# Sparse attention and a maxout layer on one core: turning transfers from two queues, the first batch's key sums kept apart, weights by quarters, a new order of the work

## The chip, the core and the metric

The kernel runs on one core of a Trainium2 chip. A core has five engines that run side by side, each taking its own instructions strictly in order: TensorE (PE; its weight loads are listed apart as PEld), VectorE (DVE), ScalarE (ACT), GpSimd (POOL) and SyncE (SP). Transfers between the chip's memory and the core's buffers are issued by SP, and in part by ACT, and are carried by 16 DMA engines. The metric is the device time of one execution in microseconds; lower is better.

## The reference, cut to what matters

Four batches of eight heads, 768 positions, 64 values per head. Each query sees the keys within 15 positions of its own, and beside them 24 summaries of 32 keys each (the maximum over the 32 keys, and the mean of the 32 values). The output of the attention, 512 numbers for each of 3072 positions, goes through a layer that takes the larger of two products and multiplies once more.

```python
k_sum = k.reshape(B, H, nb, block, D).max(axis=3)
v_sum = v.reshape(B, H, nb, block, D).mean(axis=3)
mask_l = np.abs(pos[:, None] - pos[None, :]) < window
scores_all = np.concatenate([where(mask_l, scores_l, -1e9), scores_s + np.log(block)], axis=-1)
a = softmax(scores_all)
x = matmul(a, concat([v, v_sum]))          # then (B*S, H*D)
out = np.maximum(x @ w1, x @ w2) @ w_out   # w1, w2: 512 x 1024, w_out: 1024 x 512
```

The kernel writes the maximum as h1 + max(h2 - h1, 0): it multiplies x by wd = w2 - w1, cuts at zero (g), and adds x times the product w1o = w1 w_out, which it forms once.

## The kernel before, in words

The unit of attention is a tile of 64 queries (16 rows further on than a multiple of 64) against 128 rows of keys: 96 neighbours and 32 rows that hold the 24 sums. Even tiles take their keys and values in one order of those rows, odd tiles in another. Two heads lie side by side (a "pair", hp 0 to 3), two pairs make a half (hp 0 or 2), and four tiles make a group (grp 0 to 2, 256 positions). Names carry batch, pair and group: "values 121" is batch 1, half 2, group 1.

For each batch and pair `prep` (L599 to L671) casts k and q to 16 bits (tile kqb), turns them so that the head dimension lies on the partitions, and places k in the tile kx with its neighbours, its sums (ks, made by a maximum on DVE) and copies of the tails. Pairs named in `turn` (22, 23, 30 to 33) are turned by a transposing transfer (L628, into kt), the others by TensorE (L624). `scores` (L673) fills a bank pair, `weigh` (L711) takes the exponential on ACT and hides what is out of the window (a multiplication on DVE; in the first batch a matrix product beforehand, "hide", L690), `values` (L741) multiplies by the values and divides (tile xs), and x is turned into xt: by TensorE in the first batch (L831), by a transposing transfer in the others (L822). `maxout` (L904) makes four "hidden" tasks of eight products each per group (L913), cuts them at zero on ACT or DVE ("relu"), and six "out" steps of four products each (L940 with w1o, L947 with w_out), whose banks a "copy out" empties before a store.

The weights: `load_w12` (L844) loads rows 0 to 255 or 256 to 511 of half of the columns of w1 and w2, forms that part of wd, and turns w1. A hidden task needs both row halves of its columns. `load_wo` loads w_out.

Everything is put on record as tasks, and a table in `CFG` sets the order in which they are written out (`given`, L247): one list of task numbers, one letter for each task's engine, and a list of the buffer slots. The order is thus by hand for each engine, nothing is reordered on the chip, and an instruction that waits holds all that stands behind it on its engine. The recording layer puts in the waits. Transfers count on eight counters in turn (DMAHW0 to DMAHW7), and a transfer waits for the one that used its counter before.

```python
if by_dma:
    op("S", 1.12, lambda e, src=src, ps=ps: nc.sync.dma_start_transpose(out=ps.ap[:], in_=src.ap[:]),
       read=[src], write=[ps], prio=prio, issue=1.24, label=f"turn {'kq'[n]}{tag}")
```

PSUM has eight banks. A hidden task or an out step that begins takes one, and starts only when the relu, the copy out or the exponential that read its last contents has run.

Of the kernel before, what the change touches and what calls it, by code (L numbers as in the profile page):

```python
# [27 lines left out]
    turn="22 23 30 31 32 33", lx="SSS", cols=True, emb=1, ep=0.5, vt=0.28, s32=0.36, raw=0, qg=0, wh=1, os=6,  # L28
)
CFG["order"] = list(map(int, """  # L30
# [204 lines left out]
def kernel(  # L235
# [32 lines left out]
    def tiles(name, n, shape, dt):  # L268
        return [const.tile(shape, dt, name=f"{name}{i}") for i in range(n)]


    banks = Ring(list(range(8)), {"kq": 2, "sc": -2, "av": -2, "mm": 4})
    bank_tile = psum.tile([128, 8, 512], F32, name="banks")

    def bank(buf, n=512, dt=F32, second=0):
# [54 lines left out]
    def fixed_parts():  # L330
# [24 lines left out]
        def clear_apart(e):  # L355

            for t in apart:
                zero(e, t[:])
# [701 lines left out]
```

## Time and profile before

| | us |
|---|---|
| median of the runs shown (three) | 165.5 (164.76 to 165.97) |
| the profiled execution | 166.2 |
| its span, first to last instruction | 164.4 |
| PE busy | 153.0 |
| DVE / ACT / POOL busy | 113.0 / 92.9 / 57.8 |

The granted TensorE clock was 1.000 over the whole span. The profiled execution took 0.7 us more than the median; 1.8 us of it lie outside the span. In the rows of the profile each line gives a start, a duration, the engine and what it did; "idle before <- X" says that the engine stood still until X had ended, and for a transfer "landing" is counted from its issue.

### The profile page before, as it was taken

How to read it: one execution, taken by the hardware profiler on the slowest of the kernel's cores; microseconds unless marked ns; L12 is line 12 of the kernel's file. 1: busy time of each engine (PE TensorE's matmuls, PEld its weight loads, DVE VectorE, ACT ScalarE, POOL GpSimd, SP SyncE). 2: the span in 40 equal slices, each digit the busy share in tenths (PEclk: the TensorE clock that was granted, in tenths of full speed). 3: DMA queues.
4: the chain of work that ended last, by engine and by line, in shares of the span. 5: the costliest groups of instructions: out<-in, count | busy, mean ns of one | idle time of the engine just before them, and what ended most of it. 6: DMA issues, size and time to landing. Idle time of an engine off the chain costs nothing.

```text
span 164.4 us, 4431 instructions
## 1 busy us (share of the span) xinstructions
PE 153.0 (93%) x1793; PEld 100.2 (61%) x1812; DVE 113.0 (69%) x224; ACT 92.9 (57%) x134; POOL 57.8 (35%) x91
## 2 busy tenths in 40 slices
PE   5889978999999999999999999999899999999992
PEld 2346657998565644575687646678545467766651
DVE  3698898579856899994989986569746654163221
ACT  3469995794577698836996645283937312012010
POOL 6058757302242385534672546034630000000000
PEclk9999999999999999999999999999999999999999
DMA  5999999999999999999979997997999996311015
GB/s 157 289 331 303 273 386 383 383 382 371 274 190 289 271 233 219 130 232 136 201 169 229 228 209 162 121 261 150 220 245 335 319 174 167 58 64 70 0 66 189
DMA packets 67700, 36.46 MB, mean 222 GB/s; under 512 B 54624, under 2 KB 61664, under 8 KB 67680
## 3 DMA queue, kind: packets, MB, share of 16 engines
q1 hardware_dynamic: 66208, 33.76, 87.6%
q10 hardware_dynamic: 1472, 2.43, 4.4%
q8 instruction: 14, 0.23, 0.6%
q14 instruction: 6, 0.05, 0.1%
HBM read 25.17 MB, written 6.29 MB: 191 GB/s over the span
## 4 chain that ended last, share of the span: by engine, by line
PE 62%; DMA 14%; DVE 11%; issue 4%; SPq 4%; ACT 2%; POOL 1%; ACTq 0%; POOLq 0%; DVEq 0%
PE banks L913 19%; PE banks L947 17%; PE banks L940 10%; DMA land<-in_k_dram 8%; DMA out_dram<-o 6%; PE banks L897 4%; PE banks L624 3%; PE banks L757 3%; DVE vx L593 3%; PE banks L701 2%; PE banks L982 2%; DVE ks L650 2%; DVE pb L725 2%; DVE kqb L593 1%; SPq L428 1%
## 5 line engine op out<-in xcount | busy, mean ns | idle before, releaser
L913 PE MATMUL banks<-xt,wd 128*128 128x256 bf16 x384 | 45.9, 273 | 0.1
L947 PE MATMUL banks<-wo,g 128*128 128x512 bf16 (+2 forms) x194 | 43.4, 362 | 1.8 <-issue 1.6
L913 PEld LDWEIGHTS <-wd 128*128 128x128 bf16 x384 | 37.3, 98 | 7.8 <-issue 0.5
L947 PEld LDWEIGHTS <-g 128*128 128x128 bf16 x208 | 18.7, 98 | 17.3
L715 ACT ACTIVATE pb<-banks 128x1024 bf16<-128x1024 f32 x24 | 23.6, 1026 | 6.2 <-PE banks L701 3.8
L940 PE MATMUL banks<-w1o,xt 128*128 128x512 bf16 (+2 forms) x100 | 23.5, 362 | 0.2
L922 ACT ACTIVATE g<-banks 128x512 bf16<-128x512 f32 x27 | 15.2, 604 | 7.6 <-PE banks L913 7.6
L924 DVE TENSOR_SCALAR g<-banks 128x512 bf16<-128x512 f32 x21 | 14.1, 686 | 7.8 <-PE banks L913 7.6
L816 DVE TENSOR_TENSOR xs<-banks,inv 128x512 bf16<-128x512 f32 x24 | 16.0, 686 | 4.9 <-DMA xt<-xs 4.4
L593 POOL COPY vx<-sums 32x792 bf16<-32x792 bf16 x15 | 14.7, 983 | 12.5 <-ACT sums L593 7.0
L725 DVE TENSOR_TENSOR pb<-pb,mask 128x1024 bf16<-128x1024 bf16 (+1 forms) x24 | 16.4, 710 | 4.0 <-ACT pb L715 3.7
L593 ACT COPY o<-banks 128x512 f32<-128x512 f32 (+1 forms) x8 | 4.4, 546 | 25.6 <-PE banks L947 21.1
L593 POOL CAST kqb<-land 128x768 bf16<-128x768 f32 x9 | 8.9, 985 | 20.1 <-DMA land<-in_q_dram 9.8
L940 PEld LDWEIGHTS <-xt 128*128 128x128 bf16 x104 | 9.9, 98 | 9.4
L650 DVE TENSOR_REDUCE ks<-kx 128x24 bf16<-128x768 bf16 x16 | 15.0, 945 | 0.2
L593 DVE COPY o<-banks 128x512 f32<-128x512 f32 (+2 forms) x10 | 6.2, 621 | 10.2 <-PE banks L947 8.7
L593 POOL CAST vx<-land 128x768 bf16<-128x768 f32 x10 | 8.9, 889 | 10.2 <-DMA land<-in_v_dram 10.2
L593 ACT CAST kqb<-land 128x768 bf16<-128x768 f32 x11 | 10.3, 943 | 3.2 <-DMA land<-in_k_dram 2.5
L593 DVE CAST kqb<-land 128x768 bf16<-128x768 f32 x12 | 7.0, 590 | 7.1 <-DMA land<-in_k_dram 4.7
L624 PE MATMUL banks<-ident,kqb 128*128 128x128 f32 x60 | 9.7, 278 | 1.4 <-DVE kqb L593 1.1
L757 PEld LDWEIGHTS <-pb 128*64 128x64 bf16 (+1 forms) x384 | 8.0, 110 | 4.9 <-issue 2.8
L757 PE MATMUL banks<-vx,pb 128*64 128x65 bf16 (+1 forms) x384 | 9.5, 196 | 1.3 <-DVE xs L816 0.8
(87 smaller groups left out, 183.1 us busy)
## 6 DMA issues: line engine op xcount, KB each, us to landing
land<-in_k_dram SPq DMA_DIRECT2D x16, 384.0 KB, 6.0
land<-in_v_dram SPq DMA_DIRECT2D x16, 384.0 KB, 6.9
land<-in_q_dram SPq DMA_DIRECT2D x16, 384.0 KB, 5.9
land<-in_moe_w_dram SPq DMA_DIRECT2D x8, 512.0 KB, 9.6
land<-in_moe_w_out_dram SPq DMA_DIRECT2D x4, 512.0 KB, 10.0
out_dram<-o SPq DMA_DIRECT2D x7, 256.0 KB, 4.0
out_dram<-o ACTq DMA_DIRECT2D x4, 256.0 KB, 2.8
out_dram<-w1t SPq DMA_DIRECT2D x3, 256.0 KB, 3.4
```

Source lines behind the costliest of these rows:

```text
L593: {"D": nc.vector.tensor_copy, "A": nc.scalar.copy, "P": nc.gpsimd.tensor_copy}[e](out=o, in_=i)
L624: nc.tensor.transpose(out=bank(ps)[:, 128 * j:128 * j + 128], in_=src.ap[:].bitcast(F32)[:, 128 * j:128 * j + 128], identity=ident32[:])
L650: op("D", 0.95, lambda e: nc.vector.tensor_reduce(out=ks.ap[:, 0:nb], in_=free(kt(), 128, [256, NM], [192, 2], [32, 2], [1, 32]), axis=AX. ...
L715: op("A", {"A": 1.03}, lambda e: nc.scalar.activation(out=spread(pb.ap[:, 0, 0:1], [192, 8], [128, 2], [1, 64]) if PW > 128 else spread(pb ...
L725: nc.vector.tensor_tensor(out=o, in0=o, in1=spread(mask[:, 2 * u:2 * u + 1, 0:1], [0, n], [64, 2], [1, 64]), op=ALU.mult)
L757: nc.tensor.matmul(out=o, lhsT=p[r], rhs=vx[b].ap[r, par, hp + n, 2 * grp + u, a, 0:D + 1], start=(PW == 128 or par == 0), stop=(last and ...
L816: op("D", 0.69, lambda e: nc.vector.tensor_tensor(out=x.ap[:].rearrange("p n u a d -> p n (u a) d"), in0=spread(bank_tile[:, ps.ap, 0:1], ...
L913: nc.tensor.matmul(out=bank(ps)[:, 256 * s:256 * s + 256], lhsT=wd_tile[:, quarter, c, 128 * s:128 * s + 128], rhs=x.ap[:, c, :], start=(c ...
L922: nc.scalar.activation(out=o, in_=bank(ps), func=ACT.Relu)
L924: nc.vector.tensor_scalar_max(out=o, in0=bank(ps), scalar1=0.0)
L940: nc.tensor.matmul(out=bank(ps, c1 - c0), lhsT=x.ap[:, c, sl], rhs=w1o[c].ap[:, cols], start=(c == 0), stop=False)
L947: nc.tensor.matmul(out=bank(ps, c1 - c0), lhsT=g.ap[:, f, sl], rhs=wo[f // 2].ap[:, f % 2, cols], start=False, stop=(f == FC - 1))
```

## The change

Four things change together with the table of the order.

1. **Turning transfers from ACT.** The transposing transfers for k and q (L628) and for x (L822) may be issued by ACT instead of SP. The new letters give ACT 11 of the 30: six of x and five of k and q.
2. **First batch.** Keys are placed in one run of 768 columns plus a tail of 32, with no copies of the tails and no copies of the sums. The sums are multiplied apart: after a group's 96-row products, `scores` adds products with ks into rows 96 to 127 of the same banks. Odd tiles use the same order of rows as even ones, so one tile `apart` holds the sums of the values where two did, and one mask without the odd form (hide0) does for them.
3. **First weights by quarters.** Of the four parts of w1 and w2, parts 1 and 3 become a quarter of the columns with all 512 rows each (`load_w12_quarter`), so a hidden task of these columns needs one part. Parts 0 and 2 stay halves of rows.
4. **A new order, new engines and new slots** for all tasks. Beside these, several options come in switched off (`f32`, `mx1`).

```diff
-    turn="22 23 30 31 32 33", lx="SSS", cols=True, emb=1, ep=0.5, vt=0.28, s32=0.36, raw=0, qg=0, wh=1, os=6,
+    turn="22 23 30 31 32 33", lx="SSS", cols=True, emb=1, ep=0.5, vt=0.28, s32=0.36, raw=0, qg=0, wh=2, os=6, f32="", ft=0.7, mx1=0, ksep=1, sd=0.56,
...
-44 32 2 0 3 10 12 1 4 6 11 15 13 8 112 20 30 26 56 25 46 113 116 9 122 7 123 126 14 47 16 117 34 118 132 168 28 23 133
+5 10 11 8 0 9 17 13 3 6 2 1 21 26 45 56 33 24 27 126 14 18 118 46 35 34 127 31 12 119 29 23 130 122 110 120 121 32 174
...
-                op("S", 1.12, lambda e, src=src, ps=ps: nc.sync.dma_start_transpose(out=ps.ap[:], in_=src.ap[:]),
+                op("S", {"S": 1.12, "A": 1.12}, lambda e, src=src, ps=ps: queue(e).dma_start_transpose(out=ps.ap[:], in_=src.ap[:]),
...
+        apart_k = CFG["ksep"] and b == 0
...
-            pairs(128, 192, 64), order(kps, [1, 128], [128, 6]) if by_dma else order(kps, [2, 128], [256, 3], [1, 2])),
+            kt()[:, 0:S] if apart_k else pairs(128, 192, 64), order(kps, [1, 128], [128, 6]) if by_dma else order(kps, [2, 128], [256, 3], [1, 2])),
...
+        if not apart_k:
+            copy(tail_on, {"D": 0.26, "P": 0.51, "A": 0.55}, lambda: (
+                pairs(192, 64, 32), pairs(320, 64, 32)),
+               read=[kmain, kwrap, ks], write=[kx[b, hp], tailed], prio=prio, label=f"tails k{tag}")
...
+            for n in range(2 if apart_k else 0):
+                c0 = GT * grp + 16
+                for c, at, size in ((c0, 0, min(GT, S - c0)), (0, S - c0, GT - S + c0)):
+                    for a in range(2 if size > 0 else 0):
+                        r = slice(64 * a, 64 * a + 64)
+                        nc.tensor.matmul(out=bank(ps, second=a)[96:128, GT * n + at:GT * n + at + size],
+                                         lhsT=ksum[b, hp + n].ap[r, 0:32], rhs=q_of(n, r, c, c + size), start=False,
+                                         stop=(n == 1 and at + size == GT))
...
-            op("S", 0.76, lambda e: nc.sync.dma_start_transpose(
+            op("S", {"S": 0.76, "A": 0.76}, lambda e: queue(e).dma_start_transpose(
...
+    def load_w12_quarter(n, prios, prio, prio_t):
+        at_q = n // 2
+        cols, fs = slice(256 * at_q, 256 * at_q + 256), []
+        for w, at in zip((moe_w1, moe_w2), prios):
+            f = Buf(land)
+            fs.append(f)
+            op("S", 1.47, lambda e, f=f, w=w: nc.sync.dma_start(
+                out=landed(f, KC, 256), in_=w.rearrange("(c p) n -> p c n", p=128)[:, :, cols]),
+               write=[f], prio=at, label=f"load w{n}")
...
-            op("T", 0.87, lambda e, hid=hid: hid(), read=[x, wd[n % 2], wd[n % 2 + 2]], write=[ps], prio=prio, label=f"hidden {b}{grp}{n}")
+            op("T", 0.87, lambda e, hid=hid: hid(), read=[x, wd[n]] if CFG["wh"] == 2 and n % 2 else [x, wd[n % 2], wd[n % 2 + 2]], write=[ps], prio=prio, label=f"hidden {b}{grp}{n}")
```

What the new order does at three places follows. In the rows, tiles carry their buffer's number; the brackets name what an instruction waits for, DVE, PE, Pool and Activation being counters of those engines.

**The first weights on POOL.** Before, POOL casts the last two values of the first batch (vx from land), moves single rows (vx from vx), writes one "all sums" (vx from apart) and then forms wd; each wd waits for its two loads:

```order
L593 COPY kx_82<-kx_82 128x6x2x32 [waits Pool_49]
L593 CAST vx_94<-land_69 128x2x6x64 [waits DMAHW2_49]
L593 COPY vx_94<-vx_94 32x2x64 [waits Pool_49]
L593 CAST vx_94<-land_70 128x2x6x64 [waits DMAHW3_49]
L593 COPY vx_94<-vx_94 32x2x64 [waits Pool_49]
L593 COPY vx_94<-apart_99 32x528 [waits DVE_49]
L856 TENSOR_TENSOR wd<-land_62,land_65 128x2x2x256 [waits DMAHW5_49,DMAHW4_49,Pool_49]
L856 TENSOR_TENSOR wd<-land_64,land_63 128x2x2x256 [waits DMAHW7_49,DMAHW6_49,DMAHW0_49]
```

Now, from the cast of the last value to the third part of wd:

```order
L609 CAST vx_94<-land_69 128x2x6x64 [waits DMAHW3_49,Pool_49]
L609 COPY vx_94<-vx_94 32x2x64 [waits Pool_49]
L609 COPY vx_94<-vx_94 32x10x64
L609 COPY vx_94<-apart_98 32x528 [waits Activation_49] x2
L609 COPY vx_94<-apart_98 32x528 [waits DVE_49]
L609 COPY vx_94<-apart_98 32x528
L950 TENSOR_TENSOR wd<-land_65,land_62 128x1024 [waits DMAHW5_49,DMAHW4_49,Pool_49]
L950 TENSOR_TENSOR wd<-land_63,land_64 128x1024 [waits DMAHW7_49,DMAHW6_49,DMAHW0_49]
L917 TENSOR_TENSOR wd<-land_67,land_66 128x2x2x256 [waits DMAHW2_49,DMAHW1_49,DMAHW0_49]
```

POOL writes seven "all sums" before the first wd now (four of them behind the cast of the last value, three between the cast of the last q and that of the value, which are not shown), where it wrote five; the first two wd are quarters of the columns, and three parts of wd are POOL's where two were. The task order puts the cast of the last q on POOL too.

**Turning transfers about the end of batch 1 and the keys of batch 2.** Before, SP issues all of them; each waits for its data and for its own counter (xt from xs is x of batch 1, kt from kqb are keys and queries of batch 2):

```order
L822 DMA_TRANSPOSE xt_114<-xs_111 128x4x128 [waits DMAHW2_49,DVE_49,PE_49]
L822 DMA_TRANSPOSE xt_114<-xs_109 128x4x128 [waits DMAHW3_49,DVE_49,PE_49]
L628 DMA_TRANSPOSE kt_103<-kqb_75 128x6x128 [waits DMAHW4_49,Activation_49]
L628 DMA_TRANSPOSE kt_104<-kqb_76 128x6x128 [waits DMAHW5_49,Pool_49]
L428 DMA land_62<-in_k_dram 128x2x384 [waits DMAHW6_49,DMAHW0_49,Pool_49]
L628 DMA_TRANSPOSE kt_105<-kqb_77 128x6x128 [waits DMAHW7_49]
```

Now ACT has one of them, "xt 120", between a relu (g) and the "copy out 001" (into w1t, whose space is used for outputs by then):

```order
L1011 ACTIVATE g_120<-banks 128x512 [waits PE_49]
L883 DMA_TRANSPOSE xt_115<-xs_112 128x4x128 [waits DMAHW5_49,DMAHW4_49,DMAHW6_49,DMAHW3_49,DMAHW7_49,DMAHW2_49,DVE_49]
L609 COPY w1t_126<-banks 128x512
L609 COPY vx_95<-vx_95 32x2x660 [waits Activation_49]
L609 COPY vx_95<-sums_96 32x792
L776 ACTIVATE pb_89<-banks 128x1024 [waits PE_49]
L659 DMA_TRANSPOSE kt_106<-kqb_76 128x6x128 [waits DMAHW0_49,Pool_49]
```

The six counters are those of the six turning transfers that SP issues ahead of it, the last of them "turn q23"; the recording layer makes each switch of queue wait until the other queue's turning transfers have landed.

**Keys of batch 3.** Before, ACT has the relus of batch 2 there, and no transfer that anything waits for:

```order
L593 COPY kx_79<-kt_103 128x6x2x64
L958 DMA out_dram<-w1b_124 128x512 [waits DMAHW6_49,DVE_49]
L593 COPY kx_80<-kt_104 128x6x2x64 [waits DMAHW5_49]
L922 ACTIVATE g_119<-banks 128x512 [waits PE_49] x2
L922 ACTIVATE g_120<-banks 128x512 [waits PE_49]
L593 COPY kx_80<-kx_80 128x32 [waits Activation_49]
```

Now ACT issues "turn k33", runs "copy out 101" and "copy out 121" (into w1t and w1b), issues "turn q33", and then come the relus 211 and 200:

```order
L1011 ACTIVATE g_120<-banks 128x512 [waits DVE_49,PE_49]
L659 DMA_TRANSPOSE kt_105<-kqb_76 128x6x128 [waits DMAHW3_49,DMAHW4_49,DMAHW2_49,DMAHW7_49,DMAHW1_49,DVE_49]
L609 COPY w1t_126<-banks 128x512
L609 COPY w1b_124<-banks 128x512
L659 DMA_TRANSPOSE kt_107<-kqb_77 128x6x128 [waits DMAHW0_49,DVE_49]
L1011 ACTIVATE g_121<-banks 128x512 [waits PE_49]
L1011 ACTIVATE g_120<-banks 128x512
```

Turn k33 waits for four transfers that SP issues, xt 221, xt 222, turn k30 and xt 202; turn q33 waits for turn q32, which SP issues and which itself waits for turn k33.

More of the change, by code (lines that the diff above doesn't have):

```diff
@@ L405, in fixed_parts, with wrap_first @@
         op("P", 1.65, lambda e: make_hide(), write=[half[0]], prio=-9, label="hide")
+        tripled = Buf(Ring([None]))
+        def wrap_first(e):
+            on(e).memset(hide0[0:64, 2, 48:64], NEG)
+            on(e).memset(hide0[64:96, 2, 0:48], NEG)
+        if uni:
+            op("D", {"D": 0.17, "P": 0.3}, lambda e: on(e).tensor_copy(
+                out=hide0[:], in_=spread(hide[:, 0, 0:1], [0, 3], [1, 64])), read=half[:1], write=[tripled], prio=-8, port=True,
+               label="hide first")
+            op("D", {"D": 0.16, "P": 0.28}, lambda e: wrap_first(e), read=[tripled], write=[hide0_in], prio=-8, label="hide first wrap")
         for n in range(2):
@@ L516, in spread_v @@
                               **({"S": (1.05, 0.46, 0.12)[i]} if late else {})},
-                 lambda r=r, m0=m0, m1=m1, shift=shift: (runs(r, 1, m0, m1), runs(r, 0, m0 + shift, m1 + shift)),
+                 lambda r=r, m0=m0, m1=m1, shift=shift: (
+                     runs(slice((r.start + 64) % 128, (r.start + 64) % 128 + r.stop - r.start) if uni and not late else r, 1, m0, m1),
+                     runs(r, 0, m0 + shift, m1 + shift)),
                  read=[*src, *before], write=[*out, took, done], prio=prio, label=f"odd v{tag}{i}")
@@ L602, in prep, with turn_wide @@
         tag = f"{b}{hp}"
-        pss = []
+        pss, wide = [], [f"{n}{tag}" in CFG["f32"] for n in "kq"]
         for n, eng in enumerate((k_on,) if CFG["qg"] and b == 0 else (k_on, q_on)):
             by_dma = f"{b}{hp}" in CFG["turn"]
+            if wide[n]:
+                f, ps = kqin[b, hp, n], Buf(banks, "kf")
+                pss.append(ps)
+                def turn_wide(f=f, ps=ps):
+                    for j in range(J):
+                        nc.tensor.transpose(out=spread(bank_tile[:, ps.ap, 128 * j:128 * j + 1], [1, 128])
+                                            if j < 4 else bank(ps, second=1)[:, 128 * (j - 4):128 * (j - 3)],
+                                            in_=landed(f, 2, J * D)[:, :, D * j:D * j + D], identity=ident32[:])
+                op("T", CFG["ft"], lambda e, turn=turn_wide: turn(), read=[f], write=[ps], prio=prio, label=f"turn {'kq'[n]}{tag}")
+                continue
             f, src, ps = kqin[b, hp, n], Buf(kqb), Buf(ktr) if by_dma else Buf(banks, "kq")
```

122 lines of the change are left out of this document (80 added, 42 removed), and 72 rows, old and new, of the table turn.

## The prediction

> **What bounds the kernel now.** I read the stretches first, cut where the rows of TensorE change character.
>
> ```profile
> 0.00:29.10 29.10, 23.98 (x363) 14.87 (x364) 22.44 (x65) 19.59 (x28) 17.69 (x36) 1.00 1.04 304
> 29.10:161.20 132.10, 129.06 (x1432) 85.28 (x1448) 90.30 (x161) 73.26 (x107) 40.09 (x55) 1.00 0.91 205
> 161.20:164.40 3.20, 0.00 (x0) 0.00 (x0) 0.28 (x1) 0.03 (x1) 0.00 (x0) 1.00 0.50 167
> ```
>
> The columns are the length, then busy time of PE, PEld, DVE, ACT and POOL, the granted clock, and DMA. From 29.1 to 161.2 us TensorE stands still for only 3.0 us of 132.1. So the end is the moment at which this dense run starts, plus the work in it, plus what stands still in it. ACT is busy 73.3 us of these 132.1, so it has room for more work, but not for standing still at a place where TensorE needs a bank emptied. Next, the timeline of TensorE where the run starts, and of POOL before it.
>
> ```profile
> 27.92 0.68 PE L831 MATMUL banks<-identity,xs 128*128 128x128 bf16 x9 [0.66 <-issue]
> 28.72 0.55 PE L624 MATMUL banks<-ident,kqb 128*128 128x128 f32 x3
> 29.11 2.78 PE L913 MATMUL banks<-xt,wd 128*128 128x256 bf16 x24
> ```
>
> ```profile
> 18.72 1.03 POOL L593 CAST vx<-land 128x768 bf16<-128x768 f32 x1 [0.20 <-DMA land<-in_v_dram]
> 19.81 0.28 POOL L593 COPY vx<-vx 32x128 bf16<-32x128 bf16 x1
> 22.94 2.36 POOL L856 TENSOR_TENSOR wd<-land,land 128x1024 bf16<-128x1024 f32 x1
> 25.49 2.36 POOL L856 TENSOR_TENSOR wd<-land,land 128x1024 bf16<-128x1024 f32 x1 [0.18 <-DMA land<-in_k_dram]
> ```
>
> The last value of the first batch has landed at 18.7. The second row half of the weights is there at 25.5, its wd at 27.85, and the last turns of x run to 28.6: the first hidden task (29.11) stands right behind all of that.
>
> For the counting below I take PE's own pace from the chain of waits: eight hidden products 0.87, four of an out step 0.86, three values tasks 0.89 (0.30 each), two scores tasks 0.57, the sums 0.46, a turn of k or q 0.33.
>
> ```profile
> 38.35 0.33 PE banks L624 x3
> 69.62 0.89 PE banks L757 x48
> 70.52 0.46 PE banks L569 x24
> 77.16 0.86 PE banks L947 x4
> 78.42 0.87 PE banks L913 x8
> 81.02 0.57 PE banks L701 x32
> ```
>
> **The first batch and the quarters.** Removed for each of four pairs: a copy of tails and one of sums (0.25 to 0.51 us each on DVE, ACT or POOL) and one of two copies of summed values. Added on TensorE: 32 products with ks over six scores tasks, 16 of 256 columns, 8 of 240, 8 of 16. No row shows one; the 128x256 product of L913 runs eight in 0.87, 0.11 each, so at most 24 x 0.11 + 8 x 0.03 = 2.9 us if one runs after the other, and about 1.5 if the two halves of the rows overlap as the 64-row products of L701 do (0.57 / 32 = 0.018 each for 64 columns, where 0.11 / 4 would be 0.027). All six lie ahead of the first hidden task, beside ACT's and POOL's chain, so I cost them at nothing; without that cover they cost 1.5.
>
> The twelve loads of the first batch still go ahead of the weights, so the last value still lands near 18.7. What is new is POOL's queue: after the cast of the last q it writes three "all sums", casts the last value, moves two rows, writes four more, and forms wd.
>
> ```profile
> L593 POOL COPY vx<-apart 32x528 bf16<-32x528 bf16 x5 | 3.7, 737 | 2.6 <-DVE apart L593 2.4
> L593 POOL COPY vx<-vx 32x640 bf16<-32x640 bf16 x1 | 0.7, 710 | 0.2 <-ACT vx L593 0.2
> 14.52 1.91 ACT L593 CAST kqb<-land 128x768 bf16<-128x768 f32 x2
> ```
>
> The last q had landed by 15.5, when the second of these casts starts before; on POOL the cast takes 1.0 (page row of POOL's casts, below), so it ends about 16.5, or 17 with a wait. Then 2 x 0.28 + 3 x 0.74 = 2.8 gives 19.6, the cast of v 1.03 gives 20.6, two rows 1.0 and four sums 3.0 give 24.6, and wd 2.36 gives 27.0. The first hidden task needs this quarter alone and starts near 27.1, not 29.1; the third needs the second quarter, ready at 27.0 + 2.36 = 29.4. By 29.5 two hidden tasks are done (1.74), where before none was done at 29.11; before had one turn of k behind it already (0.33). The lead is 1.74 - 0.33 - 0.4 = **1.0 us**. If the quarter could be formed as soon as its data is there (22.9), the lead would be up to 2.5; if the apart products are not covered, it is lost and 0.5 with it. The quarter loads have 1 KB runs where 2 KB stood; no row separates these, and the stretch's DMA share is above 1 either way.
>
> **Eleven turning transfers on ACT.** The order shows the wait that this adds: at each change between the two queues the later transfer waits until the other queue's have landed, and what stands behind it on ACT waits too. Before has one queue and no such wait. Its prices are these.
>
> ```profile
> L822 SPq DMA_TRANSPOSE xt<-xs x18: 1188/1264/2510, 65.8 to 139.5; - x18
> DMA to landing us min/median/max: 2.5/4.2/5.8
> L628 SPq DMA_TRANSPOSE kt<-kqb x12: 1209/1232/2094, 73.7 to 121.6; - x12
> DMA to landing us min/median/max: 2.7/2.8/4.1
> ```
>
> To issue one costs SP 1.24; on ACT none is shown. ACT's nearest row is a plain store, 0.36, so 11 cost 4 to 14 us of ACT's queue; I take SP's 1.24, as it is the same operation. By itself that is hidden in ACT's idle time. The landing is what counts. Further durations:
>
> ```profile
> L816 DVE TENSOR_TENSOR xs<-banks,inv 128x512 bf16<-128x512 f32 x24 | 16.0, 686 | 4.9 <-DMA xt<-xs 4.4
> L650 DVE TENSOR_REDUCE ks<-kx 128x24 bf16<-128x768 bf16 x16 | 15.0, 945 | 0.2
> L813 DVE RECIPROCAL inv<-banks 128x8 f32<-128x8 f32 x24 | 4.2, 191 | 5.5 <-PE banks L757 5.4
> L593 DVE COPY kx<-kt 128x768 bf16<-128x768 bf16 x4 | 3.3, 824 | 0.0
> L593 POOL CAST kqb<-land 128x768 bf16<-128x768 f32 x9 | 8.9, 985 | 20.1 <-DMA land<-in_q_dram 9.8 <-DMA land<-in_k_dram 9.6 <-POOL vx L593 0.6
> L593 DVE CAST kqb<-land 128x768 bf16<-128x768 f32 x12 | 7.0, 590 | 7.1 <-DMA land<-in_k_dram 4.7 <-DMA land<-in_q_dram 1.9 <-POOL kqb L593 0.5
> L593 ACT COPY o<-banks 128x512 f32<-128x512 f32 x7 | 4.1, 586 | 24.0 <-PE banks L947 19.5 <-DMA out_dram<-o 4.5
> L922 ACT ACTIVATE g<-banks 128x512 bf16<-128x512 f32 x27 | 15.2, 604 | 7.6 <-PE banks L913 7.6
> L593 ACT CAST vx<-land 128x768 bf16<-128x768 f32 x5 | 4.2, 835 | 3.2 <-DMA land<-in_v_dram 3.2
> ```
>
> *Place A, xt 120.* ACT may issue it only when turn q23 has landed, and copy out 001 behind it frees the bank that hidden 122 takes (by the table of slots). Count from the end of values 100. On DVE, in its order: three inv 0.57, x 122 0.69, sums 0.28, x 100 0.69, max k20 0.95, tails 0.25, place q20 0.55, relu 0.69, x 120 0.69, max k21 0.95, together 6.3. POOL then writes the sums of k21 (0.5) and casts q23 (0.99): 7.8. Turn q23 lands 2.7 later, 10.5; ACT's issue 1.24 and the copy 0.59 make 12.3. TensorE has from there to hidden 122: sums 0.46, out 001 0.86, a turn 0.33, hidden 112, 110, 111, 113 and 121 4.35, four steps of out 110 and 111 3.44, two scores 0.57: 10.0. It stands still **2.3 us**. With kt's longest landing it is 3.7; nothing, if POOL takes q23 earlier than this order lets it.
>
> *Place B, turn k33 and turn q33.* Count from the end of values 200: x 200 0.88 on DVE, xt 200 lands 2.5, ACT issues turn k32 1.24, casts two v 1.67, issues xt 220 1.24, and xt 201 lands 2.5. Only then may SP issue xt 221, xt 222, turn k30 (3 x 1.24) and xt 202, landing 2.5: 16.25. Now ACT may issue turn k33, which lands after 2.7; SP's turn q32 waits for it and lands 2.7 later; ACT issues turn q33 1.24 and runs relus 211 and 200, 1.2: 24.1. Hidden 223 takes the bank of hidden 200. TensorE has from values 200 to there 12 out steps 10.4, 9 hidden tasks 7.85, five values 1.5, two scores 0.57, sums 0.46: 20.8. It stands still **3.3 us** (1.4 of it already at hidden 210, behind copy out 121). With xt's median landing at three steps it is 8.4; nothing, if SP need not wait for xt 201 and the two k and q landings come as early as the standstill asks, 3.3 us sooner.
>
> Of the other switches the closest is xt 301: between values 301 and hidden 311 TensorE has three values 0.9 and four out steps 3.44, 4.3, against inv and x 0.88 and a landing of 2.5, 3.4. I cost these at nothing; with the median landing they cost 0.8 each.
>
> [...]
>
> **Sum.** 166.2 for the profiled execution, - 1.0 for the front, + 2.3 + 3.3: 170.8. It was 0.7 above the median, so 170.1.
>
> **Rivals.** *The waits are hidden.* At A this is so if POOL can cast q23 2.3 us sooner than DVE's and POOL's queues give it, at B if SP's four transfers go out 3.3 us sooner; then the front's lead is all that is left: 165.5 - 1.0 = 164.5, down to 163.0 with 2.5. For it speaks that ACT has 59 us without work in the dense run; against it that A and B stand where banks are short. *One place costs, the other does not:* 165.5 - 1.0 + 2.3 or + 3.3, 166.8 to 167.8. *The front is later:* the first hidden task is held by POOL's queue (24.6 for its last sum, before 22.85) and by the uncovered products; with both places still hidden that is 165.5 + 0.5 to 1.5, 166 to 167. *SP is relieved:* with 11 issues less, loads start earlier. SP waits for data far more than it issues, as this row of its waits shows, and the run has 3.0 us of standstill in all, 1.6 of it "issue", so at most 1.4 comes back: 163.1 with the lead.
>
> ```profile
> SPq L958 <- DVE o L593: 12.3, 2, 8.2
> ```
>
> **How the numbers follow.** Both places cost: 0.58, from 168 to 175, likeliest 170.1. One costs: 0.14. Front later and no more: 0.08. Hidden, with a lead between 0 and 2.5: 0.20. Of the last, 0.11 is below 163.8. Within 1% (163.8 to 167.2, about what a measurement of this kernel tells from no change) lie the rest of it, the late front and half of "one place", together 0.22; slower by over 1% 0.67. The range leaves 1 in 10 below 163.7 and 1 in 10 above 175, where B's median landings and A's longest one add up; the likeliest case by itself spans 168 to 175.
>
> **What would show it.** In the changed profile: the first L1002 row on TensorE near 27, with POOL's first wd (L950) just ahead of it; ACT idle for 2 us or more ahead of L883 and L659, released by a transfer of xt or kt; TensorE idle before L1002 or L986 by over 2 us between 75 and 85 and again between 100 and 115, released by ACT's copies of o or by g; about 9 us of standstill in the dense run instead of 3.0. The prediction is wrong if ACT's transfers show no wait, if TensorE's standstill stays near 3, or if the dense run starts before 25.5.

## The result, and the profile after

The changed kernel takes **182.8 us** (median; 181.69 to 183.61) where the kernel before takes 165.66 (164.76 to 165.97): a ratio of 1.104, 95% interval 1.097 to 1.112. The forecast was 170.1, with a range up to 175.0, so the side was right and the size was not. The profiled execution took 182.52, its span is 180.7; the same two figures of before are 166.2 and 164.4. There are 16.3 us of span to account for. In all times below, a run over 1.5% above the fastest of its own kernel (this is one run each of five kernels) is left out of the median and the range as a slow execution.

The dense stretch of the changed kernel, cut as before. The columns are length, then busy time of PE, PEld, DVE, ACT and POOL, the granted clock and DMA.

```profile
28.40:177.70 149.30, 134.74 (x1469) 86.96 (x1466) 85.84 (x166) 73.42 (x110) 44.57 (x56) 0.97 0.76 184
```

The dense run starts at 28.4 instead of 29.1 and is 149.3 us long instead of 132.1. TensorE stands still for 149.30 - 134.74 = 14.6 us of it, and it is busy 5.7 us longer, at a mean clock below 1. Of the 3.0 us that looked like standstill in before, a part was none, as the next two rows of before show (a group of instructions, and a wait of TensorE):

```profile
L947 PE MATMUL banks<-wo,g 128*128 128x512 bf16 (+2 forms) x194 | 43.4, 362 | 1.8 <-issue 1.6
PE banks L947 <- issue: 1.6, 10, 0.2
```

The program has 208 of these products, and the changed kernel's trace has all 208 (L1036). The trace of before has 194: fourteen records are missing, and their places are the ten "issue" waits. So the true standstill of before was near 3.0 - 1.6 = 1.4, and its true work near 130.7.

Where TensorE stands still now (waits of the changed kernel: us in total, times, longest):

```profile
PE banks L1002 <- ACT w1t L609: 5.7, 1, 5.7
PE banks L1002 <- ACT g L1011: 3.8, 1, 3.8
PE banks L1002 <- ACT w1b L609: 3.7, 1, 3.7
PE banks L818 <- POOL vx L609: 0.8, 1, 0.8
PE banks L1002 <- DMA xt<-xs: 0.6, 1, 0.6
```

The first three standstills, 13.2 us together, are all ahead of hidden products (L1002) whose bank ScalarE had not emptied yet (w1t and w1b are the tiles' names in the trace; what ScalarE copies there are finished outputs). The first is place A, the two others are the two halves of place B. The rows of TensorE around place A (start, us, what, and idle time before it):

```profile
80.86 0.64 PE L752 MATMUL banks<-qx,kx 64*128 64x64 bf16 x32
87.23 1.87 PE L1002 MATMUL banks<-xt,wd 128*128 128x256 bf16 x8 [5.73 <-ACT w1t L609]
88.89 3.01 PE L1036 MATMUL banks<-wo,g 128*128 128x512 bf16 x8
```

And of ScalarE at the same place:

```profile
85.28 1.27 ACTq L883 DMA_TRANSPOSE xt<-xs  x1
86.59 0.59 ACT L609 COPY w1t<-banks 128x512 f32<-128x512 f32 x1 [9.01 <-issue]
```

The reader is to see two things. ScalarE did nothing for 9.0 us ahead of the copy, because the transfer in front of it could not be issued. And TensorE's rows behind the standstill are slow by themselves: eight hidden products take 1.87 where their normal row is 1.03 to 1.04, eight products of out steps 3.01 where 1.89 is normal (both normal rows stand with the filled standstills, below). These slow rows are no wait; they are a lower clock (0.50 granted from 84.31 to 91.14), which comes below.

The 16.3 us are then: start of the dense run -0.7; standstill 14.6 - 1.4 = +13.2; slow clock +3.7 (my estimate: half of the 7.3 us that TensorE worked at a clock of 0.50, worked out below); other work +0.3 (134.74 - 130.7 - 3.7); end of the span -0.2.

### The profile page after: what moved, and what is told of

It is laid out like the page before. It is cut to its first block, busy times and chain, and to the rows that moved or that the text cites. A ratio compares the mean times of both kernels' runs of the same rounds, so it can differ in the third digit from the quotient of the medians.

```text
span 180.7 us, 4521 instructions
## 1 busy us (share of the span) xinstructions
PE 160.0 (89%) x1844; PEld 103.1 (57%) x1844; DVE 103.0 (57%) x210; ACT 93.2 (52%) x138; POOL 63.6 (35%) x90
## 4 chain that ended last, share of the span: by engine, by line
PE 71%; DMA 17%; POOL 4%; ACT 3%; issue 2%; ACTq 1%; DVE 1%; SPq 0%; POOLq 0%; DVEq 0%
PE banks L1002 20%; PE banks L1036 18%; PE banks L1029 9%; DMA kt<-kqb 6%; DMA land<-in_v_dram 4%; PE banks L818 4%; PE banks L1071 4%; PE banks L986 4%; DMA xt<-xs 4%; PE banks L752 3%; DMA land<-in_q_dram 3%; POOL vx L609 3%; PE banks L655 3%; PE banks L741 1%; PE banks L762 1%
## 5 line engine op out<-in xcount | busy, mean ns | idle before, releaser
L1002 PE MATMUL banks<-xt,wd 128*128 128x256 bf16 x384 | 46.4, 276 | 13.7 <-ACT w1t L609 5.7
L1002 PEld LDWEIGHTS <-wd 128*128 128x128 bf16 x384 | 37.5, 99 | 21.9 <-issue 14.1
L1036 PE MATMUL banks<-wo,g 128*128 128x512 bf16 (+2 forms) x208 | 48.0, 374 | 0.0
L1011 ACT ACTIVATE g<-banks 128x512 bf16<-128x512 f32 x32 | 18.3, 600 | 28.4 <-PE banks L1002 11.0
L1036 PEld LDWEIGHTS <-g 128*128 128x128 bf16 x208 | 19.3, 100 | 19.3 <-issue 1.9
L1013 DVE TENSOR_SCALAR g<-banks 128x512 bf16<-128x512 f32 x16 | 11.0, 690 | 28.3 <-PE banks L1002 28.2
L609 POOL CAST kqb<-land 128x768 bf16<-128x768 f32 x13 | 12.4, 953 | 34.3 <-DMA land<-in_k_dram 10.5
L877 DVE TENSOR_TENSOR xs<-banks,inv 128x512 bf16<-128x512 f32 x24 | 16.3, 687 | 3.7 <-DMA xt<-xs 3.3
L609 ACT COPY o<-banks 128x512 f32<-128x512 f32 (+2 forms) x13 | 7.0, 549 | 16.5 <-PE banks L1036 12.7
L786 DVE TENSOR_TENSOR pb<-pb,mask 128x1024 bf16<-128x1024 bf16 (+1 forms) x24 | 13.3, 592 | 2.0 <-ACT pb L776 1.9
L609 POOL COPY vx<-vx 32x640 bf16<-32x640 bf16 (+4 forms) x12 | 9.7, 814 | 13.5 <-ACT vx L609 11.1
L874 DVE RECIPROCAL inv<-banks 128x8 f32<-128x8 f32 x24 | 4.9, 205 | 11.2 <-PE banks L818 9.7
L609 ACT COPY w1t<-banks 128x512 f32<-128x512 f32 (+1 forms) x4 | 2.8, 698 | 15.7 <-issue 14.5
L1071 PE MATMUL banks<-identity 128*128 128x512 bf16 x28 | 9.4, 467 | 1.6 <-DVE identity L331 1.6
```

What stands on the lines that cost most here:

```text
L609: {"D": nc.vector.tensor_copy, "A": nc.scalar.copy, "P": nc.gpsimd.tensor_copy}[e](out=o, in_=i)
L786: nc.vector.tensor_tensor(out=o, in0=o, in1=spread(mask[:, 2 * u:2 * u + 1, 0:1], [0, n], [64, 2], [1, 64]), op=ALU.mult)
L877: op("D", 0.69, lambda e: nc.vector.tensor_tensor(out=x.ap[:].rearrange("p n u a d -> p n (u a) d"), in0=spread(bank_tile[:, ps.ap, 0:1], ...
L1002: nc.tensor.matmul(out=bank(ps)[:, 256 * s:256 * s + 256], lhsT=wd_tile[:, quarter, c, 128 * s:128 * s + 128], rhs=x.ap[:, c, :], start=(c ...
L1011: nc.scalar.activation(out=o, in_=bank(ps), func=ACT.Relu)
L1013: nc.vector.tensor_scalar_max(out=o, in0=bank(ps), scalar1=0.0)
```

## The experiments

The line numbers of the kernels below are one or a few higher than those of the changed kernel. The numbers in the edits are those of the tasks that issue the turning transfers; a letter S or A in the table of engines lets SyncE or ScalarE issue one. Where nothing else is said, what is computed is unchanged.

**All thirty on SyncE.**

```diff
+CFG["engines"] = "".join("S" if i in (291, 384, 494, 405, 373, 503, 505, 457, 485, 517, 531) else c for i, c in enumerate(CFG["engines"]))
```

> The changed kernel with all 30 turning transfers issued by SyncE again; order, first batch and quarters stay as changed. Theory (the switches between the two queues hold TensorE): the waits at hidden 122, 210 and 223 (5.7, 3.7 and 3.8 us) go, and with them the low clock behind them (about 4.4 us); the dense run has then 130.3 us of work (129.06 of before and 1.24 by the new order) and some 3 us of standstill, from 28.4 on: a span of about 165 and a time of 165 to 168. Rival (the order written anew, or the first batch, holds TensorE): the standstill stays over 10 us and the time at 178 or more. In between, 170 to 176: the in-order queue of SyncE holds part of it by itself.

Measured: 170.2 us (168.89 to 170.5), ratio to before 1.026 (1.019 to 1.033). Its waits of TensorE begin with these:

```profile
PE banks L1003 <- DMA xt<-xs: 1.7, 1, 1.7
...
PE banks L1037 <- issue: 1.3, 8, 0.2
PE banks L753 <- DMA kt<-kqb: 1.2, 1, 1.2
```

All three standstills are gone and the granted clock of the dense run is 1.00 in this profile (the mean clock of the four runs is 0.99 to 1.00). So 12.6 of the 17.1 us come from the eleven transfers; 4.5 remain, outside the 165 to 168 that I gave. Here the dense run is 135.6 us long with 129.4 of PE busy, 6.2 apart, of which 1.5 are "issue" gaps at missing records: 4.7 us of standstill against 1.4 before. It lies at the last batch (scores waiting for a turned k or q 1.2, hidden products waiting for xt 1.7) and at a POOL row (0.8). The POOL row is in the changed kernel too. With one queue these waits remain; which part of the change makes them was not tried.

**All thirty on ScalarE.** The same line with the letter A for all thirty: one queue, no change of queue.

> The changed kernel with all 30 turning transfers issued by ScalarE: one queue, no switch, but 30 issues of 1.2 us in ScalarE's order. If the cost lies in the switches alone, the time is as with all on SyncE, 165 to 169. If it lies in ScalarE having to wait, in order, for the data of each transfer and to issue it, ahead of copies and relus that free TensorE's banks, the time is 172 or more, with waits of TensorE on ScalarE at several places, each of 1 to 3 us.

Measured: 173.88 us (173.22 to 174.1), ratio 1.047 (1.041 to 1.053). Its waits of TensorE:

```profile
PE banks L1037 <- ACT g L1012: 1.8, 1, 1.8
PE banks L1003 <- ACT sums L610: 1.8, 1, 1.8
```

So ScalarE's strict order costs by itself, some 3.7 us for thirty transfers. That is less than a third of the 12.6 us that eleven transfers cost when they alternate with SyncE's.

**Part of the eleven back on SyncE.** First xt 120 and turn q22 (place A):

```diff
+CFG["engines"] = "".join("S" if i in (291, 384) else c for i, c in enumerate(CFG["engines"]))
```

> The changed kernel with two of the eleven transfers, xt 120 and turn q22, back on SyncE; nine stay on ScalarE. Theory: the 5.7 us ahead of hidden 122 go and the low clock that follows (1.0 us on the next eight hidden products, about 1.1 on the eight after) goes with them: 182.5 - 5.7 - 2 = 174.8, between 173.5 and 176.5; the two places near 117 and 124 stay. Rival (TensorE would have waited there for something else that is as late): under 3 us gained, 179 or more.

Then turn k33 and turn q33 (place B), the same line with (503, 505):

> The changed kernel with turn k33 and turn q33 back on SyncE; nine stay on ScalarE. Theory: the waits ahead of hidden 210 and hidden 223 (3.7 and 3.8 us) go and the low clock that follows the second (about 2 us): 182.5 - 9.5 = 173.0, between 172 and 176, since xt 220 and turn k32 still switch there; the 5.7 us ahead of hidden 122 stay. Rival (SyncE's own order holds k33 and q33 as long): under 3 us gained, 179 or more.

And the reverse of the first, xt 120 and turn q22 alone on ScalarE, the other nine on SyncE:

> The changed kernel with only xt 120 and turn q22 issued by ScalarE; the other nine are back on SyncE. Theory (xt 120 waits for turn q23, which SyncE issues after its own transfers): the wait of 5.3 to 5.8 us ahead of hidden 122 is there with its slow rows (some 2 us), so 170.2 + 7 = 177, between 175.5 and 179. Rival (the wait is made by the other nine, or what follows makes it up): 173 or less.

Measured: place A back on SyncE 179.4 us (177.75 to 179.73); place B back on SyncE 181.79 (180.51 to 182.93); place A alone on ScalarE 175.1 (175.1 to 177.23).

Place A by itself costs 175.1 - 170.2 = 4.9 us, a little under what I expected, and its trace has the wait ahead of hidden 122 (5.4). The other nine by themselves cost 179.4 - 170.2 = 9.2. The two make 14.1 where both together cost 12.6; the difference of 1.5 is smaller than the spread of the runs, so it is not shown that one place costs more alone than beside the others. But my expectations for the first two kernels were wrong, both by their rival's number: taking place A away gave back 3.4 us and not 7.7, taking place B away 1.0 and not 9.5. The traces show that other waits come in their stead. With place A back on SyncE, its wait is gone and those of place B are 2.8 and 2.4, but scores tasks wait 1.8 for turned keys and sums 1.6 for values, where the changed kernel has no such wait. With place B back on SyncE, this wait of TensorE is new (beside place A's, 5.3):

```profile
PE banks L753 <- DMA kt<-kqb: 4.8, 3, 2.2
```

The two waits of place B are gone, and three waits of scores tasks (L753) for turned keys stand in their stead: with k33 and q33 on SyncE the last batch's turns of k and q still alternate with xt transfers of ScalarE (fourteen changes of queue instead of eighteen), each waits for the one before, and the batch's scores are late instead of the banks.

**Filling the standstills.** Products that no result uses, into empty banks, ahead of hidden 122 (position 441 of the order) and hidden 223 (position 591):

```diff
+def keep(b, n):
+    for _ in range(n):
+        nc.tensor.matmul(out=bank_tile[:, b], lhsT=identity[:], rhs=wo[0].ap[:, 0, :], start=True, stop=True)
+plan.ahead = {441: lambda: keep(2, 18), 591: lambda: keep(3, 16)}
```

> The changed kernel with products added on TensorE that no result uses: 18 of 128x512 (3.9 us) ahead of hidden 122, 16 (3.5 us) ahead of hidden 223, into banks that stand empty there; the transfers and their waits stay. Theory (the granted clock falls because TensorE stood idle for 5.7 us, and for 3.7 and 3.8 us shortly after each other): the added products lie inside the standstills, the rows behind them take their normal 0.87 per eight and the clock is near 1.0; 182.5 less about 4.4, so 177.5 to 179.5. Rival (the clock falls for another reason, such as the load of the whole kernel, or the slow rows are modelled ends): the rows behind the standstills stay slow and the time stays at 181.5 to 184.

Measured: 180.09 us (179.19 to 180.82), 2.7 below the changed kernel. The rows of TensorE (L1123 are the added products):

```profile
83.11 4.04 PE L1123 MATMUL banks<-wo,identity 128*128 128x512 bf16 x18 [1.06 <-DVE g L1015]
87.42 1.03 PE L1004 MATMUL banks<-xt,wd 128*128 128x256 bf16 x8 [0.26 <-ACT w1t L611]
88.29 1.89 PE L1038 MATMUL banks<-wo,g 128*128 128x512 bf16 x8
...
117.96 5.32 PE L1004 MATMUL banks<-xt,wd 128*128 128x256 bf16 x32 [2.14 <-ACT w1b L611]
123.12 3.62 PE L1123 MATMUL banks<-wo,identity 128*128 128x512 bf16 x16
126.57 1.04 PE L1004 MATMUL banks<-xt,wd 128*128 128x256 bf16 x8
127.44 1.03 PE L1038 MATMUL banks<-wo,g 128*128 128x512 bf16 x4
```

The changed kernel has this row at the place of the last one:

```profile
128.70 1.91 PE L1036 MATMUL banks<-wo,g 128*128 128x512 bf16 x4
```

TensorE starts hidden 122 no earlier (87.42, unfilled 87.23), but its eight products now take 1.03 and not 1.87, and the four of the out step behind hidden 223 take 1.03 and not 1.91. So the slow rows are the idle time's doing, not the load's. The time fell less than the 3.3 to 5.3 us I gave because the clock now fell at a third place: at hidden 210, unfilled in both kernels, 32 products take 5.32 after a standstill of 2.14 us, where the changed kernel ran them in 3.65 after one of 3.70. That odd pair is the subject of the last section.

**The same eleven transfers in the old order.** The kernel before, with a choice of queue at its two lines that issue turning transfers, and the same eleven on ScalarE:

```diff
+CFG["engines"] = "".join("A" if i in (394, 301, 504, 415, 513, 383, 515, 467, 495, 527, 541) else c for i, c in enumerate(CFG["engines"]))
```

> The kernel before, with the same eleven turning transfers issued by ScalarE at their places in its own order; nothing else of the change. Theory (the switches between the queues cost by themselves): it loses 8 us or more, 174 to 185, with ScalarE idle by several us ahead of its rows behind the transfers and TensorE idle behind copies and relus of ScalarE; the loss need not be the changed kernel's, since the order differs. Rival (the old order has room for the switches and the new one has not): 165 to 169.

Measured: 187.81 us (186.28 to 188.13), ratio 1.130 (1.122 to 1.139): 22.2 us more than before, above the upper end of what I expected. Its two longest waits of TensorE:

```profile
PE banks L941 <- ACT sums L594: 5.1, 1, 5.1
PE banks L914 <- DMA xt<-xs: 3.0, 1, 3.0
```

The rival falls: the old order has no room for these transfers on ScalarE either, and pays more for them than the new one (22.2 against 12.6).

**Copies ahead of the transfers.** All eleven stay on ScalarE; xt 120 goes behind copy out 001, turn k33 behind copies out 101 and 121, turn q33 behind relus 211 and 200:

```diff
+for t, behind in ((291, 560), (503, 650), (505, 653)):
+    order.remove(t)
+    order.insert(order.index(behind) + 1, t)
```

> The changed kernel with all eleven transfers still on ScalarE, but three of them moved behind the work that they held: xt 120 behind copy out 001, turn k33 behind copies out 101 and 121, turn q33 behind relus 211 and 200. Theory (TensorE stands still because copies and relus are queued on ScalarE behind a transfer that waits): the waits of 5.7, 3.7 and 3.8 us ahead of hidden 122, 210 and 223 go; some comes back where the transfers' own data is wanted, above all ahead of hidden 101, which needs xt 120 (4.35 us of TensorE's work later, so some 2 to 3 us of wait there); 174 to 179. Rival (the data of the transfers, not what is queued behind them, holds TensorE): under 2 us gained, 181 or more.

And the first of these moves alone, with only xt 120 and turn q22 on ScalarE:

> Only xt 120 and turn q22 on ScalarE, the other nine on SyncE, and xt 120 moved behind copy out 001. Theory (what is queued behind the waiting transfer holds TensorE): no wait ahead of hidden 122, 2 to 3 us ahead of hidden 101 instead, and the clock may stay full: 171 to 174, where the same split with the transfer ahead of the copy gave 176.2. Rival: 175.5 or more.

Measured: 184.85 us (184.28 to 186.1) for the first, 175.8 (173.82 to 176.34) for the second, where the same split without the move gave 175.1. My theory of that moment falls. The rows of TensorE of the second kernel show how:

```profile
84.19 1.91 PE L1007 MATMUL banks<-xt,wd 128*128 128x256 bf16 x16
89.80 0.38 PE L1007 MATMUL banks<-xt,wd 128*128 128x256 bf16 x2 [3.70 <-ACT pb L781]
91.98 4.42 PE L1007 MATMUL banks<-xt,wd 128*128 128x256 bf16 x20 [1.80 <-DMA xt<-xs]
```

Hidden 122 no longer waits, and TensorE runs on for 4.5 us. Then it stands still for 3.70 until ScalarE has run what is now queued behind the transfer (a row of exp, which frees a bank of scores), and 1.80 more until xt 120 itself has landed: 5.5 us, as much as at the old place. The bank was only the first of three things that the held transfer delays; the others came due less than 5 us later.

**The last eleven on ScalarE.** The same number of transfers on ScalarE, but the last eleven of the thirty: one change of queue instead of eighteen.

```diff
+CFG["engines"] = "".join("S" if i in (291, 384, 494, 405, 373, 503) else c for i, c in enumerate(CFG["engines"]))
+CFG["engines"] = "".join("A" if i in (496, 505, 464, 466, 457, 524, 485, 478, 517, 531, 492) else c for i, c in enumerate(CFG["engines"]))
```

> The changed kernel with eleven turning transfers on ScalarE as before this run, but the last eleven of the thirty in the order of the program: one change of queue instead of eighteen. Theory (the number of changes of queue sets the cost, not the number of transfers on ScalarE): near the kernel with all on SyncE (170.2), more by one wait at the change and by the issues on ScalarE (all thirty there cost 3.7): 170 to 174, with a full clock. Rival (eleven transfers on ScalarE cost by their place in its order, whatever the changes): 178 or more.

Measured: 175.9 us (175.44 to 176.77), 6.9 less than with the same number scattered, and 1.9 above the upper end that I gave. The largest wait of TensorE, and POOL's row behind it:

```profile
PE banks L1004 <- ACT g L1013: 6.5, 1, 6.5
```

```profile
115.99 0.82 POOL L611 CAST kqb<-land 128x768 bf16<-128x768 f32 x1 [5.84 <-DMA land<-in_k_dram]
```

All its extra time lies at one standstill of 6.5 us and the slow clock behind it (0.50 for 6.8 us). By the trace it is not the change of queue that makes it: that change held ScalarE's first transfer, turn q32, until 113.67, but turn k31, which ScalarE is to issue ahead of two relus, turns what POOL casts at 115.99, as soon as its keys have landed, and could not have gone before 116.8. ScalarE stands there in order for late data; no run moves turn k31 alone. Behind it, eight transfers of ScalarE and no change of queue cost nothing that the trace shows. So the number of changes of queue is not the measure either; what cost here was a transfer that could not start yet, ahead of work that TensorE needed (6.5 us of standstill).

**The quarters.** In the kernel with all thirty on SyncE, the first weights by halves again:

```diff
-    raw=0, qg=0, wh=2
+    raw=0, qg=0, wh=1
```

> All 30 transfers on SyncE, and the first weights by halves as before instead of by quarters; the rest as changed. If the quarters are what lets the first hidden task start ahead of the second POOL difference, it starts 2.0 to 2.5 us later without them, near 30.5, and the time goes from 170.2 to 171.5 to 172.5. If the front gains nothing from them (by the end of the first product of the weights the changed kernel had no lead), the time stays within 0.7 of 170.2.

And the other way round, the kernel before with the quarters (the new function, its call, and the two lists of what waits for what):

```diff
-            op("T", 0.87, ..., read=[x, wd[n % 2], wd[n % 2 + 2]], ...
+            op("T", 0.87, ..., read=[x, wd[n]] if CFG["wh"] == 2 and n % 2 else [x, wd[n % 2], wd[n % 2 + 2]], ...
-        load_w12(n, ...
+        (load_w12_quarter if CFG["wh"] == 2 and n % 2 else load_w12)(n, ...
```

> The kernel before with the first two parts of the weights loaded by quarters, and nothing else of the change. In its profile the first hidden task stands behind the last copies of xt (DVE, to 28.78) and behind turns of x and k on TensorE up to 29.27, not behind the second POOL difference (27.85) alone. By that the quarters bring under 0.5 us: 165.2 to 166.2. If the second difference was what held the start, 164 to 165, a kernel faster than both.

Measured: 171.6 us (171.33 to 171.95) without quarters where 170.2 was with them; 165.35 (164.07 to 166.21) for the kernel before with quarters, ratio 0.998 (0.994 to 1.001). In the new order the quarters seem worth some 1.4 us: the intervals of the two ratios, 1.026 to 1.043 and 1.019 to 1.033, overlap, so the times alone don't show it, but the trace agrees. Without them the first hidden task waits for POOL's second difference and starts at 29.62 and not 28.36:

```profile
29.62 1.05 PE L1003 MATMUL banks<-xt,wd 128*128 128x256 bf16 x8 [1.08 <-POOL wd L918]
```

In the old order they change nothing that can be measured; the first hidden task still stands behind the turns of x and k there (29.4 in its profile). No kernel here is shown to be faster than the one before.

## Why the prediction was wrong in size

The sum gave 170.8 us for the profiled execution, which took 182.5. Nearly all of these 11.7 us are in four terms: 3.4 are the size of the wait at place A, 4.2 that at place B, 3.7 a slow clock, and 0.3 the front. So the steps that failed are the terms of the two waits, which were too short, and a clock taken for full without a reason; the waits themselves were the right ones.

*What bounds the kernel: right.* The end is the start of the dense run, plus work, plus standstill, and 13.2 of the 16.3 us lost are standstill. The 3.0 us of standstill that I read were too many by 1.6, since "issue" there was missing records.

*The front, forecast lead 1.0: about 0.4.* POOL did what was forecast (last of its sums near 24.3, forecast 24.6; first wd from 24.43, ready at 26.8, forecast 27.0):

```profile
21.81 2.53 POOL L609 COPY vx<-apart 32x528 bf16<-32x528 bf16 x4
24.43 4.66 POOL L950 TENSOR_TENSOR wd<-land,land 128x1024 bf16<-128x1024 f32 x2
```

But the first hidden task came at 28.4, not 27.1. The step that failed is "I cost them at nothing" for the 32 products with ks: from 14 us on, the chain that ends last is TensorE's own rows, and the new line L762 has 12.3% of the 16 us between 14 and 30, which is 2.0 us. I had given 1.5 without cover; nothing covered them, and POOL's early difference lay ready for 1.6 us. That the start would have come 2.0 earlier without these products is read from the chain; no run leaves them out. Of the start that is 0.7 earlier, the 0.3 of added work is to be taken off: turns of w1 and x now lie between the first hidden tasks, where before had done all its turns of x and two of the four of w1 by 29.11:

```profile
28.25 1.04 PE L1002 MATMUL banks<-xt,wd 128*128 128x256 bf16 x8
29.12 0.61 PE L960 MATMUL banks<-identity,w1b 128*128 128x128 bf16 x8
29.57 0.39 PE L892 MATMUL banks<-identity,xs 128*128 128x128 bf16 x4
```

*The issue on ScalarE, taken as 1.24: right.* The nearest row that I had otherwise was 0.36.

```profile
L659 ACTq DMA_TRANSPOSE kt<-kqb x5: 1227/1227/1528, 86.7 to 138.0; - x5
L883 ACTq DMA_TRANSPOSE xt<-xs x6: 1204/1211/1273, 85.3 to 159.7; - x6
```

*Place A, forecast 2.3: 5.7. The mechanism was right, the size was off by 3.4.* The term that failed is the 10.5 us from the end of values 100 (71.35 in this trace) to turn q23's landing. POOL's cast of q23 ended at 80.05, 0.9 later than the 7.8 that I counted. But SyncE's queue was not in the sum. Its rows there:

```profile
77.86 2.68 SPq L659 DMA_TRANSPOSE kt<-kqb  x1
80.60 1.26 SPq L883 DMA_TRANSPOSE xt<-xs  x1
82.04 1.95 SPq L659 DMA_TRANSPOSE kt<-kqb  x1
```

Turn k23 and xt 100 stand ahead of turn q23, so it went out at 82.04, 2.0 after its data was there, and landed 3.2 later, not 2.7: 0.9 + 2.0 + 0.5 = 3.4. The place's 2.3 would have needed SyncE free at 80.05.

*Place B, forecast 3.3: 7.5.* The chain is the one that I named, as the chain that ended last shows:

```profile
115.37 2.48 DMA xt<-xs
...
118.03 4.52 DMA kt<-kqb
...
122.61 2.73 DMA kt<-kqb
...
125.42 1.23 ACTq L659
...
127.83 1.07 PE banks L1002 x8
```

xt 202, then turn k33, turn q32, turn q33's issue, and behind two relus hidden 223: each landing waits for the one before it. The mis-sized terms are the 16.25 us from the end of values 200 (99.06) to k33's issue, which took 19.0, and k33's landing, 4.52 for 2.7. Of the 2.7 us in the first term, 1.2 are xt 200, which went out at 101.13, 2.07 behind values 200 and not 0.88, and about 1.5 are xt 201, issued at 107.31, behind which SyncE could go on at 111.45 only, 4.1 later for 2.5. Of the place's wait 3.7 us stood at hidden 210, where I had put 1.4. With "xt's median landing at three steps" I had given 8.4 for the place as its upper end. That the place came near it is luck: one xt landing of the three was that long, and the two others (xt 202 above) were near 2.5. I had taken the shortest landings that before shows. k33's transfer went out behind two loads that SyncE had issued at 116.64 and 117.31, turn q32's 2.73 stood behind none; that the loads made the difference was not tried.

*The other changes of queue, forecast nothing: right.* Of the others the trace shows one wait of 0.6, where 0.8 was the most I gave for xt 301.

*A slow clock, not forecast at all: 3.7.* The sum took TensorE's rows at their pace of before all through. With the front and places A and B taken at their true size it would have been 166.2 - 0.7 + 5.7 + 7.5 = 178.7. The rest to 182.5 is the clock.

*The rivals.* "The waits are hidden" and "one place costs, the other does not" are refuted by the three waits; the late front is not seen, though its uncovered products are. "SP is relieved" gives nothing that shows: SyncE with eleven transfers less still waits for data (its turning transfers of k and q, L659, wait 9.1 us for a landing of the other queue). That the later transfer at a change of queue waits until the other queue's have landed, as the changed kernel's order has it, is what the trace shows: turn q23, issued at 82.04, landed 3.2 later, and xt 120 went out at 85.28. The runs put the price of the eleven transfers at 12.6 us here.

*The forecast's marks.* ScalarE stood idle for 9.0, 5.5 and 6.3 us at a transfer that waited, where "2 us or more" was the mark; TensorE's waits stood at 81.5 to 87.2 (forecast 75 to 85) and at 116.7 and 124.1 (forecast 100 to 115); the standstill was 14.6, not about 9.

What stays open is how the remaining 4.5 us of the kernel with all thirty on SyncE divide between the apart products, the new order of DVE and POOL, and SyncE's load in the last batch; only the quarters were tried alone.

## What to carry to other kernels

Where a program holds the transfers of one queue until those of the other have landed, as the recording layer does here, every change of queue turns independent transfers into a chain (place B's runs from xt 202 at 115.37 to the end of turn q33's issue at 126.65), so count the chain with the issuing queue's own backlog and not with the shortest landings that a trace of one queue shows. An engine that issues a transfer early in its order holds all that is queued behind it (ScalarE stood idle for 9.0 us at xt 120) and also the transfer's own readers, so letting one of these go first may only move the standstill, as it did here from hidden 122 (5.4 us) to the tasks 4.5 us later (5.5 us). And a standstill of TensorE can be dearer than its length: behind the 5.73 us at place A it worked for 3.9 us at a clock of 0.50, of which some 2 us are lost by my estimate.

## What the runs showed of the clock

I had not expected that the clock would fall at one standstill and not at a longer one. In the traces of the nine kernels whose clock fell the low clock is 0.50, and it comes in spells of 3.41 or 6.83 us (in the changed kernel from 84.31 to 91.14 and from 128.68 to 132.09); within one kernel the falls are 44.4, 27.3, 64.9 and 37.5 us apart, which is 13, 8, 19 and 11 times 3.41. So I cut the runs into windows as long as the short spell that begin or end at a fall. The changed kernel, TensorE's view (stretch, length, busy time, clock):

```profile
80.90:84.31 3.41, 0.60 (x33) 1.00 1.03 156
84.31:87.72 3.41, 0.49 (x3) 0.50 0.77 220
87.72:91.14 3.42, 3.42 (x13) 0.50 1.20 212
115.03:118.44 3.41, 1.69 (x16) 1.00 0.63 107
118.44:121.85 3.41, 1.43 (x14) 1.00 1.15 270
...
125.27:128.68 3.41, 0.85 (x8) 1.00 0.29 58
128.68:132.09 3.41, 3.41 (x10) 0.50 0.73 67
```

And the kernel with the filled standstills:

```profile
114.69:118.10 3.41, 1.27 (x13) 1.00 0.79 181
118.10:121.51 3.41, 3.41 (x18) 0.50 0.70 121
```

The standstill of 3.70 us at hidden 210 fell across two windows, with 1.72 and 1.98 us of idle time, and the clock stayed; the one of 2.14 in the other kernel lay within one window, and the clock halved for the next. In the windows of those nine kernels, from 34 us to about the end of their dense runs, every window ahead of a fall had 2.14 us of idle time or more, and no window at full clock with 1.98 or less was followed by one; the kernels with all on SyncE and all on ScalarE, whose longest standstills in the dense run are 1.7 and 1.8 us, show a clock of 1.00 up to the last 3.0 us of their spans. Back at 0.50, the clock returned after windows with up to 0.72 us of idle time and not after those with 1.22 or more. TensorE's work at half clock in the changed kernel was 91.14 - 87.23 = 3.9 and 3.4 us, 7.3 together, of which half, 3.7, is lost by my estimate (eight hidden products took 1.87 there for 1.03).

So the length of a standstill alone did not decide it here: 2.14 us in one window were enough and 3.70 across two were not. The mean granted clock of the changed kernel's four runs lies between 0.962 and 0.972, so by my estimate two executions of one kernel can differ by part of such a spell; that this makes the spread of the changed kernel's times was not tried.
